# w_in in one load, wo in four, x in five pieces and a mask used as a view, in a single-token attention and gated-MLP kernel

## The chip, the cores and the metric

The kernel runs on one core of a Trainium2 chip. The metric is device microseconds of one execution; lower is better. Three executions of the kernel before gave 126.82 to 126.93 us, median 126.91.

## The reference

One token `x` of 576 features is normalized, and two branches read it; both are added to `x`.

```python
xn = layernorm(x)                                   # [1, 1, 576]
# A: attention over the last W = 4096 positions of a cache
q = (xn @ wq).reshape(1, 1, 32, 128)                # 32 query heads
k, v = k_cache[:, :, -4096:, :], v_cache[:, :, -4096:, :]   # 16 heads, each for two query heads
a = softmax(q @ k.T * 128 ** -0.5) @ v
A = a.reshape(1, 1, 4096) @ wo                      # wo [4096, 576]
# B: gated MLP
z = gelu(xn @ w_in)                                 # w_in [576, 4608]
z1, z2 = z[..., :2304], layernorm(z[..., 2304:])
B = (z1 * (w_sp * z2 + b_sp)) @ w_out               # w_out [2304, 576]
out = x + A + B
```

All inputs are bf16. The window of K and V is 32 MiB, and with the four weight matrices the kernel reads 50.96 MB.

## The kernel before

The order of the instructions on each engine is the order in which the code issues them (`tc.manual_schedule()`); semaphores are put in by the framework.

**Loads.** All big loads are issued by SP, in one order: wq (two row groups, then seven), K0, K1, w_in (seven, then two), K2, V0, K3, V1, V2, V3, w_out, wo in five pieces. K and V are loaded in four groups of four heads, 4 MiB each, 32,768 bytes on each of the 128 partitions. The weights are seen as half rows: `rows(slot, src, name, lo, n, at)` (L74) loads `n` row blocks per partition from block `lo`, either into a new tile of the pool `big` with the tag `slot`, or (with `at`) into part of a tile that is there. Four tags, `a` to `d`, are four buffers, each as large as the largest tile of its tag; a load into a buffer waits until all readers of the tile before it are done:

- `a`: wq's seven rows, w_in's seven rows, V1, then `ends[0]` (w_out and the last wo pieces)
- `b`: K0, K2, V2
- `c`: K1, V0, V3
- `d`: `rest` (wq's first two rows, at 4096 w_in's last two), K3, then `ends[1]` (the first wo pieces)

SP issues in order, so a load that waits holds back the loads behind it. Each load signals one of eight DMA semaphores, which are given out in turn over SP's and ACT's loads; a load waits for the last load that used its semaphore.

**x.** ACT issues the loads of `x` into `xrow` (three pieces of 192 elements, L114) and of the scalars w_sp and b_sp into `spb` (L116, L117).

**Setup.** DVE and POOL build masks from an identity. `cm` (L145) marks, per partition, two by two classes; `dmask` (L147) is the same repeated 128 times along the free dimension, 128x512 fp32, written by POOL.

**The chain from x.** DVE spreads `xrow` into `xtw` (L184) once all pieces are there, PE turns it into a column, DVE and POOL normalize it into `XT` (L209 to L212). PE multiplies wq (L220), waiting before that in its order for `spb` (L213). `qps` goes through `q_rep` (L231, L229) and L237 to `Qb` (L248).

**Groups.** For each of the four groups and each half `c`, `keys` (L264) transposes K on DVE, four instructions of 128x1024 fp32, and `scores` (L271) multiplies on PE. `sm_a` takes the maximum on DVE and the exponentials on ACT (L298), `sm_b` transposes them (L309) and copies them (ACT, L312), `pv` (L335) multiplies by V, `norm` (L345, L349) picks each head's own quarter by `dmask` and adds, `y_mms` and `y_copy` put the result into `Y`. `z_mms` (L371) multiplies w_in, in 162 small matmuls between the scores of groups 1 and 2.

**The end.** PE adds `x`, then w_out's 18 row blocks (`hv`), then wo's 32 row blocks (`Y`) into two accumulators (L471, four matmuls a row block); the group 3 result `Y` comes between w_out's second and third part. Then DVE and ACT copy the accumulators to `res`, and ACT writes it out.

Of the kernel before, what the change touches and what calls it, by code (L numbers as in the profile page):

```python
# [8 lines left out]
FP32 = mybir.dt.float32  # L9
BF16 = mybir.dt.bfloat16  # L10
ALU = mybir.AluOpType
# [3 lines left out]
D = 576  # L15
HQ = 32
HKV = 16
DH = 128
# [8 lines left out]
NR = 98  # L27
NF = FH // 128
QW = D // 4
XP = D // 3  # L30
EPS = 1e-5
SCALE = DH ** -0.5
GELU_C = 0.7978845608028654
NS = 9
# [3 lines left out]
def kernel(  # L38
# [14 lines left out]
    nc = tc.nc  # L53
    P = nc.NUM_PARTITIONS
# [4 lines left out]
    const = ctx.enter_context(tc.tile_pool(name="const", bufs=1))  # L59
# [11 lines left out]
    x_flat = A_x.flatten_outer_dims()  # L71


    def rows(slot, src, name, lo, n, at=None):  # L74

        w = src.shape[1]
        if at is None:
            t = big.tile([P, n * w], BF16, name=f"{name}{lo}", tag=slot)[:]
        else:
            t = slot[:, at:at + n * w]  # L80
        v = t.rearrange("p (s c) -> p s c", c=w)
        nc.sync.dma_start(v, src.rearrange("(p s) c -> p s c", p=P)[:, lo:lo + n, :])  # L82
        return [(lo + s, v[:, s, :]) for s in range(n)]

    def load_kv(slot, src, g, name):

        t = big.tile([P, TP * DH], BF16, name=f"{name}{g}", tag=slot)
        nc.sync.dma_start(t[:], src[0, GK * g:GK * g + GK, SK - W:SK, :].rearrange("h (r t) d -> r h (t d)", t=TP))
        return t[:].rearrange("p (t d) -> p t d", d=DH)

    wq_h = A_wq.rearrange("r (e c) -> (r e) c", e=2)
    win_h = B_w_in.rearrange("r (e c) -> (r e) c", e=2)
    K, V = {}, {}
    rest = big.tile([P, TP * DH], BF16, name="rest", tag="d")
    wq_sb = rows(rest, wq_h, "wq", 0, 2, 0) + rows("a", wq_h, "wq", 2, 7)
    K[0] = load_kv("b", A_k_cache, 0, "k")
    K[1] = load_kv("c", A_k_cache, 1, "k")
    win_sb = rows("a", win_h, "win", 0, 7) + rows(rest, win_h, "win", 7, 2, 4096)
    K[2] = load_kv("b", A_k_cache, 2, "k")
    V[0] = load_kv("c", A_v_cache, 0, "v")  # L100
    K[3] = load_kv("d", A_k_cache, 3, "k")
# [3 lines left out]
    ends = [big.tile([P, TP * DH], BF16, name=f"end{n}", tag="ad"[n]) for n in range(2)]  # L105
    wout_sb = rows(ends[0], B_w_out, "wout", 0, NF, 0)
    wo_sb = []
    for n, t, at in ((14, 1, 0), (9, 1, 14), (6, 0, NF), (2, 0, NF + 6), (1, 0, NF + 8)):
        wo_sb += rows(ends[t], A_wo, "wo", len(wo_sb), n, at * D)


    xrow = const.tile([1, D], BF16, name="xrow")
    for n in range(3):
        nc.scalar.dma_start(xrow[:, XP * n:XP * (n + 1)], x_flat[:, XP * n:XP * (n + 1)])  # L114
    spb = const.tile([1, 2], BF16, name="spb")
    nc.scalar.dma_start(spb[:, 0:1], B_w_sp.flatten_outer_dims()[0:1, 0:1])  # L116
    nc.scalar.dma_start(spb[:, 1:2], B_b_sp.flatten_outer_dims()[0:1, 0:1])  # L117
# [24 lines left out]
    cm = const.tile([P, 2, 2], FP32, name="cm")  # L142
    idc = ident[:].rearrange("p (q u y e) -> p u q y e", q=4, u=2, e=2)
    for e in range(2):
        nc.vector.tensor_reduce(out=cm[:, :, e], in_=idc[:, :, :, :, e], op=ALU.add, axis=mybir.AxisListType.XY)  # L145
    dmask = const.tile([P, 4, DH], FP32, name="dmask")
    nc.gpsimd.tensor_copy(dmask[:], cm[:].rearrange("p u e -> p (u e)").unsqueeze(2).to_broadcast([P, 4, DH]))  # L147
    ohm = const.tile([P, 8], FP32, name="ohm")
    nc.vector.tensor_reduce(out=ohm[:], in_=ident[:].rearrange("p (v y e) -> p y v e", y=8, e=2), op=ALU.add,
                            axis=mybir.AxisListType.XY)  # L150
# [17 lines left out]
    for n in range(2):  # L168
        t = ps_s.tile([P, 2, 512], FP32, name=f"S{n}")
        nc.vector.memset(t[:], 0.0)  # L170
        S.append(t)
    ops = ps_o.tile([P, 512], FP32, name="ops")
# [12 lines left out]
    for j in range(NS):  # L185
# [8 lines left out]
        out=junk[:], in0=x_col[:], in1=x_col[:], scale=1.0, scalar=0.0,  # L194
        op0=ALU.mult, op1=ALU.add, accum_out=stat[:, 1:2],
# [10 lines left out]
                            op0=ALU.subtract, op1=ALU.mult)  # L206
# [135 lines left out]
    def norm(g):  # L342
        d = st[g]
        om = work.tile([P, 4, DH], FP32, name=f"om{g}", tag="om")
        nc.vector.scalar_tensor_tensor(out=om[:].rearrange("p c d -> p (c d)"), in0=ops[:],  # L345
                                       scalar=d["rs"][:, 0:1], in1=dmask[:].rearrange("p c d -> p (c d)"),
                                       op0=ALU.mult, op1=ALU.mult)
        on = work.tile([P, DH], FP32, name=f"on{g}", tag="on")
        nc.vector.reduce_sum(on[:], om[:].rearrange("p c d -> p d c"), axis=AXX)  # L349
        d["on"] = on  # L350
# [67 lines left out]
    def tail(g):  # L418
        recip(g)
        norm(g)  # L420
        y_mms(g)
        y_copy(g)
# [17 lines left out]
    for n, pool in enumerate((ps_a, ps_b)):  # L440
        t = pool.tile([P, 512], FP32, name=f"acc{n}", tag="ab"[n])
# [77 lines left out]
```

## Time and profile before

| | |
|---|---|
| median of three executions | 126.91 us |
| profiled execution | 126.97 us, of which span 125.1 us |
| HBM read | 50.96 MB, 407 GB/s over the span |
| PE, weight loads, DVE, ACT, POOL busy | 70.2, 30.4, 78.6, 43.2, 7.2 us |
| SP's DMA queue, share of 16 DMA engines | 95.3% |
| granted TensorE clock, mean | 0.754 |

A line of the groups or of the timeline gives start and duration in microseconds, the engine, the line of the source, the operation, output and inputs, shape, and how many instructions are merged; in brackets stands the idle time ahead of it and what ended that. PEld are weight loads, which run beside matmuls. `SPq` and `ACTq` are the engines' own DMA instructions. The rows of tenths cut the span into 40 slices of 3.1 us.

### The profile page before, as it was taken

The page shows a single profiled execution, that of the slowest core. Times are in us where ns is not written, and L with a number is a line of the kernel's source. Part 1 is how long each engine was busy: PE and PEld are TensorE (multiplying, and loading weights), DVE is VectorE, ACT ScalarE, POOL GpSimd, SP SyncE. Part 2 cuts the span into 40 slices and gives each one's busy share as a digit, 9 for nine tenths or more (in the row PEclk, how much of TensorE's full clock was granted, in tenths as well). Part 3 has the DMA queues.
Part 4 walks back from the last instruction along what each step waited for, and adds up shares of the span by engine and source line. Part 5 has one row for each costly group of instructions (what it writes and reads, how often), then busy time and mean ns, then how long its engine had stood idle before and what let it go on. Part 6 is the DMA issues. An engine that isn't in the chain of part 4 may idle for free.

```text
span 125.1 us, 1826 instructions
## 1 busy us (share of the span) xinstructions
PE 70.2 (56%) x728; PEld 30.4 (24%) x728; DVE 78.6 (63%) x152; ACT 43.2 (34%) x101; POOL 7.2 (6%) x21
## 2 busy tenths in 40 slices
PE   0012841009886659999580991059892931059972
PEld 0011201001101002999100031002212311026961
DVE  6845135899699976509999367999938359003200
ACT  2100011000000974998079009608701941940000
POOL 2972000000000000000000000000000100000000
PEclk9999997555599958655568599558997555555999
DMA  4999899998999999898999989899998989999960
GB/s 113 507 422 440 363 503 409 430 482 356 498 389 433 385 482 471 377 492 341 492 430 419 471 367 487 359 482 440 409 482 356 492 374 453 414 434 409 413 248 0
DMA packets 2613, 51.06 MB, mean 408 GB/s; under 512 B 300, under 2 KB 430, under 8 KB 686
## 3 DMA queue, kind: packets, MB, share of 16 engines
q1 hardware_dynamic: 2592, 50.96, 95.3%
q8 instruction: 5, 0.08, 0.2%
q14 instruction: 2, 0.02, 0.0%
q10 hardware_dynamic: 14, 0.00, 0.0%
HBM read 50.96 MB, written 0.00 MB: 407 GB/s over the span
## 4 chain that ended last, share of the span: by engine, by line
DMA 62%; DVE 30%; PE 4%; SPq 1%; issue 1%; ACT 0%; DVEq 0%
DMA k<-in_A_k_cache_dram 36%; DMA end<-in_A_wo_dram 25%; DVE kT L264 22%; DVE pt L309 4%; PE S L271 3%; SPq L82 1%; DVE mx L292 1%; DVE on L349 1%; DVE om L345 1%; PE acc L471 0%; PE yps L356 0%; DVE rs L326 0%; ACT res L487 0%; DVE mt L281 0%; DVE mb L287 0%
## 5 line engine op out<-in xcount | busy, mean ns | idle before, releaser
L271 PE MATMUL S<-kT,Qb 128*8 128x512 bf16 x128 | 32.4, 1145 | 23.2 <-DVE kT L264 22.7
L264 DVE STREAM_TRANSPOSE kT<-k 128x1024 f32<-128x1024 f32 x32 | 36.8, 1207 | 6.2 <-DMA k<-in_A_k_cache_dram 6.2
L298 ACT ACTIVATE pz<-S,nm 32x1024 bf16<-32x1024 f32 x16 | 19.2, 1198 | 34.0 <-DVE nm L295 21.1
L312 ACT COPY PT<-pt 32x128 f32<-32x128 f32 x64 | 19.9, 311 | 16.5 <-DVE pt L309 15.8
L335 PE MATMUL ops<-v,PT 128*32 128x512 bf16 x128 | 11.0, 506 | 6.8 <-ACT PT L312 6.8
L271 PEld LDWEIGHTS <-Qb 128*8 128x8 bf16 x128 | 3.6, 96 | 44.9 <-issue 35.4
L309 DVE STREAM_TRANSPOSE pt<-pz 128x1024 f32<-128x1024 f32 x8 | 9.4, 1210 | 0.8 <-ACT pz L298 0.8
L345 DVE SCALAR_TENSOR_TENSOR om<-ops,rs,dmask 128x512 f32<-128x512 f32 x4 | 3.0, 751 | 10.5 <-PE ops L335 10.3
L371 PEld LDWEIGHTS <-win 128*128 128x128 bf16 x126 | 7.9, 166 | 2.0 <-issue 2.0
L371 PE MATMUL zps<-XT,win 128*128 128x2 bf16 x126 | 8.0, 202 | 0.0
L292 DVE TENSOR_REDUCE mx<-S 128x1 f32<-128x1024 f32 x4 | 4.9, 1216 | 4.0 <-PE S L271 3.9
L335 PEld LDWEIGHTS <-PT 128*32 128x32 bf16 x128 | 3.8, 118 | 11.4 <-ACT PT L312 6.9
L229 ACT CAST q_rep<-qps 128x512 bf16<-128x512 f32 x2 | 1.2, 585 | 14.9 <-DVE q_rep L231 14.9
L410 POOL TENSOR_TENSOR mz<-mz,mhalf 128x1 f32<-128x1 f32 x1 | 0.6, 553 | 84.9 <-DVE mz L409 84.9
L186 PE MATMUL ps_x<-ones_b,xtw 1*128 1x1 bf16 x9 | 0.4, 162 | 8.9 <-DVE xtw L184 8.9
L471 PE MATMUL acc<-end,Y 128*2 128x144 bf16 x128 | 4.5, 226 | 0.9 <-DMA end<-in_A_wo_dram 0.8
L231 DVE CAST q_rep<-qps 128x512 bf16<-128x512 f32 x2 | 1.4, 692 | 4.9 <-PE qps L220 4.2
L487 ACT CAST res<-acc 2x144 bf16<-2x144 f32 x1 | 0.3, 270 | 12.0 <-PE acc L471 12.0
L471 PEld LDWEIGHTS <-Y 128*2 128x2 bf16 x128 | 4.1, 84 | 1.2 <-issue 1.2
L356 PE MATMUL yps<-on,sel 128*32 128x32 f32 x32 | 2.0, 210 | 4.1 <-DVE on L349 4.1
L349 DVE TENSOR_REDUCE on<-om 128x128 f32<-128x512 f32 x4 | 4.2, 1043 | 0.1
L486 DVE CAST res<-acc 2x144 bf16<-2x144 f32 x1 | 0.3, 295 | 5.7 <-PE acc L471 5.7
(96 smaller groups left out, 57.6 us busy)
## 6 DMA issues: line engine op xcount, KB each, us to landing
k<-in_A_k_cache_dram SPq DMA_DIRECT2D x4, 4096.0 KB
v<-in_A_v_cache_dram SPq DMA_DIRECT2D x4, 4096.0 KB, 25.4
win<-in_B_w_in_dram SPq DMA_DIRECT2D x1, 4032.0 KB, 26.9
wq<-in_A_wq_dram SPq DMA_DIRECT2D x1, 3584.0 KB, 12.8
end<-in_B_w_out_dram SPq DMA_DIRECT2D x1, 2592.0 KB, 22.3
end<-in_A_wo_dram SPq DMA_DIRECT2D x1, 2016.0 KB
end<-in_A_wo_dram SPq DMA_DIRECT2D x1, 1296.0 KB
rest<-in_B_w_in_dram SPq DMA_DIRECT2D x1, 1152.0 KB
```

What stands on the lines that cost most here:

```text
L264: nc.vector.transpose(dst[:, 1024 * n:1024 * (n + 1)], src[:, 1024 * n:1024 * (n + 1)])
L271: nc.tensor.matmul(S[g % 2][32 * x:32 * x + 8, c, :], lhsT=Qb[:, GK * g + x, be].rearrange("p a h -> p (a h)"), rhs=kv[:, be // 2, be % 2, x],
L292: nc.vector.tensor_reduce(out=mx[:, 0:1], in_=s[:], op=ALU.max, axis=mybir.AxisListType.XY)
L298: nc.scalar.activation(pz[lo:hi, :, :, x, :], s[lo:hi].rearrange("p a (t r e) -> p (a t) r e", r=8, e=2), ACT.Exp, bias=nm[lo:hi, 0:1], sc ...
L309: nc.vector.transpose(dst[:, 1024 * n:1024 * (n + 1)], src[:, 1024 * n:1024 * (n + 1)])
L312: nc.scalar.copy(PT4[32 * a:32 * a + 32, :, x, :], pt[32 * x:32 * x + 32, :, 2 * a:2 * a + 2])
L335: nc.tensor.matmul(ops[32 * q:32 * q + 32, :], lhsT=d["PT"][:, t0 // 2:t0 // 2 + 2].rearrange("p t x h e -> p (t x h e)"), rhs=V[g][:, t0: ...
L345: nc.vector.scalar_tensor_tensor(out=om[:].rearrange("p c d -> p (c d)"), in0=ops[:], scalar=d["rs"][:, 0:1], in1=dmask[:].rearrange("p c ...
L349: nc.vector.reduce_sum(on[:], om[:].rearrange("p c d -> p d c"), axis=AXX)
L356: nc.tensor.matmul(yps[32 * g:32 * g + 32, :], lhsT=sel[:, dq, :], rhs=d["on"][:, 32 * dq:32 * dq + 32], start=(dq == 0), stop=(dq == 3), ...
L371: nc.tensor.matmul(zps[:, :, t], lhsT=wt[:, t, :], rhs=XT[:, s, :], start=(s == 0 and t == 0), stop=(s == NS - 1 and t == NF - 1), skip_gr ...
L471: nc.tensor.matmul(acc[n], lhsT=lhs[:, col, 1 - r:3 - r], rhs=wv[:, QW * (2 * r + n):QW * (2 * r + n + 1)], start=False, stop=(last and r ...
```

## The change

w_in is loaded in one load of nine row blocks into buffer `a`, which grows to 41,472 bytes per partition; `rest` then holds only wq's two rows. wo is loaded in four pieces of 19, 9, 3 and 1 row blocks, the first two into buffer `d` and the others behind w_out in buffer `a`, where five of 14, 9, 6, 2 and 1 were loaded before. `x` is loaded in pieces of 120 elements, four and one of 96. `dmask` is no tile any more but a view of `cm` with a step of zero along the 128 elements, and the product in `norm` reads that view. Nothing is computed otherwise, and the order of the instructions on each engine is unchanged but for these.

```diff
-XP = D // 3
+XP = 120
...
-    win_sb = rows("a", win_h, "win", 0, 7) + rows(rest, win_h, "win", 7, 2, 4096)
+    win_sb = rows("a", win_h, "win", 0, NS)
...
-    for n, t, at in ((14, 1, 0), (9, 1, 14), (6, 0, NF), (2, 0, NF + 6), (1, 0, NF + 8)):
+    for n, t, at in ((19, 1, 0), (9, 1, 19), (3, 0, NF), (1, 0, NF + 3)):
         wo_sb += rows(ends[t], A_wo, "wo", len(wo_sb), n, at * D)
...
-    for n in range(3):
-        nc.scalar.dma_start(xrow[:, XP * n:XP * (n + 1)], x_flat[:, XP * n:XP * (n + 1)])
+    for lo in range(0, D, XP):
+        nc.scalar.dma_start(xrow[:, lo:min(lo + XP, D)], x_flat[:, lo:min(lo + XP, D)])
...
-    dmask = const.tile([P, 4, DH], FP32, name="dmask")
-    nc.gpsimd.tensor_copy(dmask[:], cm[:].rearrange("p u e -> p (u e)").unsqueeze(2).to_broadcast([P, 4, DH]))
+    dmask = cm[:].rearrange("p u e -> p (u e)").unsqueeze(2).to_broadcast([P, 4, DH])
...
-        nc.vector.scalar_tensor_tensor(out=om[:].rearrange("p c d -> p (c d)"), in0=ops[:],
-                                       scalar=d["rs"][:, 0:1], in1=dmask[:].rearrange("p c d -> p (c d)"),
-                                       op0=ALU.mult, op1=ALU.mult)
+        nc.vector.scalar_tensor_tensor(out=om[:], in0=ops[:].rearrange("p (c d) -> p c d", c=4),
+                                       scalar=d["rs"][:, 0:1], in1=dmask, op0=ALU.mult, op1=ALU.mult)
```

## The prediction

> **What bounds the kernel now.** I read the page's slices first, then the chain that ended last, then the end of the timeline, then the trace's record of single DMA packets and semaphore landings.
>
> ```profile
> DMA  4999899998999999898999989899998989999960
> q1 hardware_dynamic: 2592, 50.96, 95.3%
> DMA k<-in_A_k_cache_dram 36%; DMA end<-in_A_wo_dram 25%; DVE kT L264 22%; DVE pt L309 4%; PE S L271 3%; SPq L82 1%; DVE mx L292 1%; DVE on L349 1%; DVE om L345 1%; PE acc L471 0%; PE yps L356 0%; DVE rs L326 0%; ACT res L487 0%; DVE mt L281 0%; DVE mb L287 0%
> ```
>
> The DMA row has no hole between the first and the last two slices, and q1 (SP's queue) fills 95.3% of 16 engines' span. The packet record makes that sharper: summed over 2.0 to 122.0 us only 0.92 us of one 16-engine stretch is idle, nearly all of it after 120 us. The chain names K's load and the transposes only because SP issued loads behind them; each load was queued well before the stream reached it. So the body is bytes over rate, and the change moves no bytes. What can move the time is the overhead per load, a hole in the stream, and what follows the last bytes.
>
> ```profile
> 117.25 2.97 PEld L471 LDWEIGHTS <-Y 128*2 128x2 bf16 x93
> 121.14 1.60 PE L471 MATMUL acc<-end,Y 128*2 128x144 bf16 x36 [0.77 <-DMA end<-in_A_wo_dram]
> 122.17 0.36 PEld L471 LDWEIGHTS <-Y 128*2 128x2 bf16 x11 [0.26 <-issue]
> 122.81 0.27 ACT L487 CAST res<-acc 2x144 bf16<-2x144 f32 x1 [11.98 <-PE acc L471]
> ```
>
> PE does 23 row blocks of wo from 117.25 in 2.97 us (0.129 each), waits for the six-row piece (landed 121.10), waits again for the two-row piece (122.13), and does the last block after 122.41, when the one-row piece lands. The engines finish unevenly: of the 16 landings of the six-row piece ten lie at 119.4 to 119.9 and four at 120.9 to 121.1. Each late engine carried one 16,384-byte packet of q8 (instruction loads, at 37.4, 57.2, 76.6, 100.7 us), which put it back some 1.4 us. The fifth, at 120.1, hits another engine, which lands last.
>
> **Two loads fewer.** w_in's 32,256 + 9,216 bytes per partition become one of 41,472, and five wo loads become four. Median landing to median landing, one load takes 9.70 us for 32,768 bytes per partition, 9.57 for 32,256, 2.73 for 9,216, 2.06 for 6,912, 0.36 for 1,152. A line through 32,768 and 1,152 leaves 0.02 us per load beyond its bytes, so two loads are worth 0.04 us. The other bound is the single packet: 1,213 ns for 32,768 bytes, 58 ns for 1,152, which leaves 16 ns a packet; eight packets per engine and load make 0.13, two loads 0.26. I take 0.04, because the landings include overlap of successive packets. No packet over 32,768 bytes is in the trace; if it were cut in two, the price is that of before, so 0.
>
> **K3 no longer waits for z_mms.** Slot d then holds only two rows of wq. K3 was issued at 59.69 and was needed when V0's bytes ended, near 65. Hidden already: zero. V1 now waits for all z_mms in slot a; it waited behind K3 for the same event.
>
> **x in five pieces.** This is the part with length. All x and spb loads go to one DMA engine, each as one data packet and one semaphore packet, and there they take turns with SP's packets.
>
> ```profile
> 0.73 1.09 ACTq L114 DMA_DIRECT2D xrow<-in_A_x_dram  x3
> 7.55 1.34 DVE L184 COPY xtw<-xrow 1x1152 bf16<-1x1152 bf16 x1 [1.42 <-DMA xrow<-in_A_x_dram]
> 11.81 0.16 PE L213 MATMUL ps_x<-spb,ones_b 1*128 1x2 bf16 x1 [1.34 <-DMA spb<-in_B_b_sp_dram]
> 23.74 9.13 DVE L264 STREAM_TRANSPOSE kT<-k 128x1024 f32<-128x1024 f32 x8 [0.51 <-DMA k<-in_A_k_cache_dram]
> 56.49 4.62 DVE L264 STREAM_TRANSPOSE kT<-k 128x1024 f32<-128x1024 f32 x4 [4.61 <-DMA k<-in_A_k_cache_dram]
> ```
>
> Packets of q10 start at 1.745 (piece 0), 4.94 and 4.96 (piece 1 and its semaphore), then one per turn, 1.065 us apart, behind one 28,672-byte packet of wq each: 6.02, 7.10, 8.17 and on to 11.36. Two more pieces are four more turns, 4 x 1.065 = 4.26 us, so x is complete at 7.42 + 4.26 = 11.68. spb's last lands near 16.2 (the last two turns behind 1.21 us packets of K), still before XT is wanted at 12.80 + 4.26 = 17.06. wq has then landed, so qps loses its 0.2 wait: Qb ends 3.9 later, at 27.1. The first transposes, which sat ready for K0 at 23.74, begin 3.4 late. Of that 1.07 goes in K1's wait (33.94 becomes 36.3), and the other 2.3 in the 4.61 us that DVE waited for K2. What is left comes through ACT: its exponentials of group 1 end at 61.4, where DVE wanted them at 61.04. From there the compute chain runs 0.35 late to the end: Y near 117.45 instead of 117.11. On the queue, K2 is issued at 36.3 (needed 45), V0 at 47.7 (55), V1 at 62 (74), wo at 89.8 (109.7): no hole.
>
> By the Trainium skill's page "DMA: Bandwidth & Descriptors", section "Queues, rings and completion order", an engine drains a whole packet of some 9 to 17 descriptors from one ring before it switches. The trace agrees for the first load alone (eight 8,192-byte packets pass before piece 1); by that rule x would be complete some 26 us late (a rival below).
>
> **Semaphores.** Eight DMA semaphores go round in program order, and a load waits for the last user of its own. With two more ACT loads, wq's seven rows wait for x's piece 0 (landed 2.06; issue to first packet is 1.0 us at the start, so its bytes are ready at 3.1, before the first load runs out at 4.92), K0 for wq's two rows (5.50; needed 13.7), K1 for piece 1 (5.46; needed 23). Nothing on the path, by 1.8 us in the nearest case.
>
> **The view of the mask.** POOL loses a copy of 0.61 us that ended 80 us before its use. The four products on DVE (751 ns for 512 fp32) read the same count with a zero step. No row has such an operand on DVE's product; bounds from 0 to, say, the reduce over a strided view, 1,043 ns: +0.3 us on Y. I take 0, the operation and the PSUM operand being the same.
>
> **The end, summed.** wo's pieces of 19, 9, 3, 1: a block costs 0.341 us of stream (2.73 / 8). The 19-row piece lands on the late engines at 115.93 + 5 x 0.341 = 117.6, about where Y is ready; PE is through it at 120.1. The 9-row piece lands at 119.04 + 1.7 = 120.75, less 0.04. PE: 36 matmuls to 121.9, twelve for the three-row piece (on the late engines at 121.8) to 122.3, the last block then or after its landing, 122.1 to 122.4 as the last q8 packet falls. End of the last matmul at 122.62 to 122.84, against 122.78: from -0.16 to +0.06, mid -0.05. With the stream's saving counted inside, I forecast -0.1: 126.97 of the profiled execution (125.1 of span and 1.87 around it) becomes 126.87, and at the median of 126.91, 0.06 lower, 126.81. A measurement here tells about 0.2%, 0.25 us, from nothing.
>
> **Rivals.**
> Faster: the packet row is right (0.26 instead of 0.04) and the fifth q8 packet, requested 0.4 us later with Y, comes after its engine is done, so the last landing is that of the other four, 122.18 instead of 122.41. Together some -0.45: 126.45. For it: the fit of packet durations is straight. Against: the landings. Chance 0.30, with lesser forms that still pass 0.25.
> Slower, x later still: PE needs 128 x 0.0323 + 0.2 = 4.3 us from Y; Y may come 0.7 us later than I have it before PE ends after the stream. If piece 1's semaphore also takes a turn of its own, x is 1.07 later, the chain is 1.4 late at the end, and the end moves to 123.0: +0.25; two turns more, +1.3. So 127.2 to 128.2. The pair at 4.94 speaks against it. Chance 0.15.
> Slower, the first wait: piece 0 went out 4 ns after the first SP packet (1.745 against 1.741). Were it caught behind the eight packets it would land near 5.3, wq would start at 6.5 instead of 4.92, and a hole of 1.5 us in the stream gives 128.4. Chance 0.06.
> Whole bursts on the ring: x complete at 33 us instead of 7.4, w_in issued near 43 and moving at 44 on a queue dry since 33, and K2, at 58.7, after w_in's end at 56.3: holes of 11 and 3.4 us, 141 us. Piece 2 at 6.02 speaks against it. Chance 0.02.
> The forecast, within 0.25 us: 0.47.
>
> So faster 0.30, same 0.47, slower 0.23. The likeliest case's own range is 126.65 to 127.1. Low end 126.4 by the faster case; the high end takes in the one-turn case and part of the next, 127.5; the first wait and whole bursts are left out.
>
> **What would show it.** Right: q10 packets of x to 10.3 us and xtw at 11.8; first transposes at 27; no slice of DMA under 8 before the end; w_in's landing 0.0 to 0.1 earlier against K1's; PE at wo in three stretches, from 117.6, 120.7 and without a wait after. Wrong: a dip in the DMA row in the second slice (the first wait), PE still on wo more than 0.6 us after the last landing (the compute chain), or a landing of the one-row piece under 122.0.

## The result, and the profile after

The changed kernel takes 127.3 us (median of 17 executions, 126.98 to 128.07) against 126.89 us (126.69 to 127.3) of the kernel before, timed beside it on the same chip. The ratio is 1.0042, with a 95% interval of 1.0025 to 1.0058: slower by 0.3 to 0.7 us. The forecast was 126.81 us, in a range of 126.4 to 127.5, no difference that could be told from nothing. The executions scatter far more than before: nine lie at 126.98 to 127.3 us, eight at 127.42 to 128.07. The profiled one is the fastest of them (126.98 us, span 125.1), so this profile shows the cause in its mildest form; an experiment below (x5_on_before) shows it in full. One execution in all the series below, of x5_on_before, took 129.28 us, over 1.5% above the fastest of its kernel, and is left out of times and ratios.

The page of the changed kernel, the rows that were shown of before:

```profile
DMA  4999998999999988998989999899998989999960
q1 hardware_dynamic: 2304, 50.96, 95.2%
DMA k<-in_A_k_cache_dram 33%; DMA end<-in_A_wo_dram 25%; DVE kT L263 22%; DMA rest<-in_A_wq_dram 4%; DVE pt L308 4%; PE S L270 3%; PE acc L469 1%; DVE mx L291 1%; DVE on L347 1%; DVE om L344 1%; PE yps L354 0%; DVE rs L325 0%; ACT res L485 0%; DVE mt L280 0%; DVE mb L286 0%
```

Between the first and the last two slices none of DMA is under 8, as before, and SP's queue has lost 288 packets (two loads of 128 data and 16 semaphore packets) without a change of its share. What is new is in the chain: `rest`, the first load of wq, with 4%. The timeline of the changed kernel shows why that load now releases something:

```profile
0.74 1.69 ACTq L114 DMA_DIRECT2D xrow<-in_A_x_dram  x5
1.97 0.33 SPq L82 DMA_DIRECT2D wq<-in_A_wq_dram  x1
5.69 1.26 SPq L88 DMA_DIRECT2D k<-in_A_k_cache_dram  x2
7.73 1.34 DVE L183 COPY xtw<-xrow 1x1152 bf16<-1x1152 bf16 x1 [1.59 <-DMA xrow<-in_A_x_dram]
11.99 0.16 PE L212 MATMUL ps_x<-spb,ones_b 1*128 1x2 bf16 x1 [1.33 <-DMA spb<-in_B_b_sp_dram]
14.89 3.15 PE L219 MATMUL qps<-wq,XT 128*2 128x512 bf16 x28 [0.88 <-DMA wq<-in_A_wq_dram]
24.55 9.13 DVE L263 STREAM_TRANSPOSE kT<-k 128x1024 f32<-128x1024 f32 x8 [0.37 <-DMA k<-in_A_k_cache_dram]
56.64 4.62 DVE L263 STREAM_TRANSPOSE kT<-k 128x1024 f32<-128x1024 f32 x4 [4.48 <-DMA k<-in_A_k_cache_dram]
```

The same two SP rows in the timeline of the kernel before, and then the waits of SP's queue in the changed kernel (time in total, how often, the longest):

```profile
1.17 0.42 SPq L82 DMA_DIRECT2D wq<-in_A_wq_dram  x1
1.64 1.30 SPq L88 DMA_DIRECT2D k<-in_A_k_cache_dram  x2
```

```profile
SPq L82 <- DMA xrow<-in_A_x_dram: 0.8, 1, 0.8
SPq L88 <- DMA rest<-in_A_wq_dram: 3.4, 1, 3.4
```

wq's seven rows are queued at 1.97 us instead of 1.17, because their semaphore is now x's piece 0's; K0 and K1 go out at 5.69 instead of 1.64, behind the end of the first load. Both waits were in the prediction, priced at nothing. The first of them is the loss, as the experiments below show.

The record of single packets shows what becomes of it. Before, wq's 128 packets of 28,672 bytes take 1,062 ns each, every one of them: 135.94 us in all. The first load's packets end at 4.84 to 5.23 on the 16 engines, and wq's begin at 4.79 to 5.23. In the changed kernel the first load's packets end at 4.89 to 5.34, but one engine takes up wq only at 5.94, and four packets take longer, up to 1.19 us. That engine stays behind: wq's slowest landing is 14.85 (median 13.88), K0's 24.53 (23.56).

In this execution it costs nothing in the end. A packet's record names no engine, but each packet starts within some nanoseconds of the end of the one before it on its engine, so an engine can be followed. The late one carries no instruction load (q8, the 16,384-byte packets of the prediction) and ends w_out at 110.38; four engines that carried one each end it at 110.76 to 110.90, and those are the last at the end.

### The profile page after: what moved, and what is told of

Same layout as the page of the kernel before. It is cut to its first block, busy times and chain, and to the rows that moved or that the text cites. A ratio compares the mean times of both kernels' runs of the same rounds, so it can differ in the third digit from the quotient of the medians.

```text
span 125.1 us, 1826 instructions
## 1 busy us (share of the span) xinstructions
PE 70.2 (56%) x728; PEld 30.3 (24%) x728; DVE 78.5 (63%) x152; ACT 43.1 (34%) x101; POOL 6.6 (5%) x20
## 4 chain that ended last, share of the span: by engine, by line
DMA 62%; DVE 30%; PE 5%; issue 1%; ACT 0%; SPq 0%; DVEq 0%
DMA k<-in_A_k_cache_dram 33%; DMA end<-in_A_wo_dram 25%; DVE kT L263 22%; DMA rest<-in_A_wq_dram 4%; DVE pt L308 4%; PE S L270 3%; PE acc L469 1%; DVE mx L291 1%; DVE on L347 1%; DVE om L344 1%; PE yps L354 0%; DVE rs L325 0%; ACT res L485 0%; DVE mt L280 0%; DVE mb L286 0%
## 5 line engine op out<-in xcount | busy, mean ns | idle before, releaser
L369 PEld LDWEIGHTS <-win 128*128 128x128 bf16 x162 | 10.1, 169 | 1.9 <-issue 1.9
L369 PE MATMUL zps<-XT,win 128*128 128x2 bf16 x162 | 10.2, 202 | 0.0
L344 DVE SCALAR_TENSOR_TENSOR om<-ops,rs,cm 128x512 f32<-128x512 f32 x4 | 3.0, 751 | 10.5 <-PE ops L334 10.3
```

Of the source, the lines that this page charges most:

```text
L344: nc.vector.scalar_tensor_tensor(out=om[:], in0=ops[:].rearrange("p (c d) -> p c d", c=4), scalar=d["rs"][:, 0:1], in1=dmask, op0=ALU.mult ...
L369: nc.tensor.matmul(zps[:, :, t], lhsT=wt[:, t, :], rhs=XT[:, s, :], start=(s == 0 and t == 0), stop=(s == NS - 1 and t == NF - 1), skip_gr ...
```

## The experiments

Each was timed in five rounds beside the kernel before, whose median lay between 126.83 and 126.94 us. Ratios are to its executions, with 95% intervals; they aren't the quotient of the two medians. "Queued" is the start of SP's DMA instruction.

### Which part of the change

**x3_on_after: three pieces of x again.** Theory: the moved semaphores are the loss; rivals: the five pieces' own packets, the wo pieces, w_in's single load.

```diff
-XP = 120
+XP = D // 3
```

> The changed kernel with x in three pieces again; all else as changed. Theory 1 (first wait): with two ACT loads fewer, wq's seven rows no longer share a semaphore with x's piece 0 and are issued near 1.2 us without a wait; the time goes back to 126.9 (126.6 to 127.1) and its spread back to that of before (some 0.6 us between lowest and highest, against 1.1). Theory 2 (the cost lies in the 41,472-byte packets of w_in or in wo's four pieces): it stays at 127.3.

126.98 us (126.84 to 127.11, 12 executions), 1.001 [1.0002, 1.0019]. Its timeline has wq back at its old place:

```profile
1.16 0.42 SPq L82 DMA_DIRECT2D wq<-in_A_wq_dram  x1
1.63 1.28 SPq L88 DMA_DIRECT2D k<-in_A_k_cache_dram  x2
```

No execution is over 127.11: the pieces of x carry the loss but for 0.1%, and the scatter with it.

**x5_on_before: only the five pieces**, in the kernel before (the diff above, reversed).

> The kernel before with x in five pieces and nothing else. Theory 1: wq waits for piece 0, as in the changed kernel; 127.3 with single executions to 128. Theory 2: no change, 126.9.

128.14 us (127.06 to 128.44, 8 executions), 1.0083 [1.0057, 1.0109]. The profiled execution took 128.19 us, with the loss in full; rows of its timeline:

```profile
1.99 0.33 SPq L82 DMA_DIRECT2D wq<-in_A_wq_dram  x1
5.48 1.25 SPq L88 DMA_DIRECT2D k<-in_A_k_cache_dram  x2
121.87 0.92 PE L471 MATMUL acc<-end,Y 128*2 128x144 bf16 x24 [0.44 <-DMA end<-in_A_wo_dram]
123.24 0.65 PE L471 MATMUL acc<-end,Y 128*2 128x144 bf16 x12 [0.45 <-DMA end<-in_A_wo_dram]
123.95 0.27 ACT L487 CAST res<-acc 2x144 bf16<-2x144 f32 x1 [12.36 <-PE acc L471]
```

PE's last twelve matmuls begin at 123.24, behind a wait for wo, and `res` follows at 123.95 (122.81 before). The loss was there from the start: the median landing of wq is 0.64 us later than before, that of K0 0.66, that of K1 0.71, and the last piece of wo lands at 123.55 instead of 122.41. What the stream loses near 5 us stays lost, because every engine carries an equal part of each later load and the one that is furthest behind ends last.

**after_spb_pool: five pieces, but the two `spb` loads on GpSimd's queue.** Its loads don't take part in the turn of the eight semaphores, so wq and K0 wait for nobody.

```diff
-    nc.scalar.dma_start(spb[:, 0:1], B_w_sp.flatten_outer_dims()[0:1, 0:1])
-    nc.scalar.dma_start(spb[:, 1:2], B_b_sp.flatten_outer_dims()[0:1, 0:1])
+    nc.gpsimd.dma_start(spb[:, 0:1], B_w_sp.flatten_outer_dims()[0:1, 0:1])
+    nc.gpsimd.dma_start(spb[:, 1:2], B_b_sp.flatten_outer_dims()[0:1, 0:1])
```

> The changed kernel, x still in five pieces, but the two scalars of spb are loaded from POOL's queue, so that ACT has five loads and wq shares no semaphore with piece 0. Theory 1: 126.9 or a little less, narrow spread. Theory 3 (five pieces cost by their own turns on the one DMA engine, not by the wait): 127.3 as changed.

127.13 us (126.93 to 127.26, 12 executions), 1.0019 [1.001, 1.0029]; wq queued at 1.17, its packets 135.99 us in all. With five pieces and without the wait the executions over 127.3 are gone. The 0.2% that is left is 0.1% more than with three pieces; here x does take its turns, and the chain from it starts nearly as late as forecast (shown in the part on the prediction). Whether that is the 0.1% isn't shown.

**wo4_on_before and wo4_again: only the four pieces of wo**, the same kernel twice.

```diff
-    for n, t, at in ((14, 1, 0), (9, 1, 14), (6, 0, NF), (2, 0, NF + 6), (1, 0, NF + 8)):
+    for n, t, at in ((19, 1, 0), (9, 1, 19), (3, 0, NF), (1, 0, NF + 3)):
```

> The kernel before with wo in pieces of 19, 9, 3 and 1 and nothing else. Theory 1: within 0.15 us of 126.9. Theory 2: up to 127.3.

126.98 us (126.77 to 128.19, 12 executions), 1.0021 [0.9999, 1.0043]; two executions were at 128.04 and 128.19. The profiled one, at 127.18, has no late load (wq queued at 1.15); the two have no trace.

> wo in 19, 9, 3 and 1 on the kernel before, a second time: two of twelve executions were at 128.0 and 128.2, the others at 126.8 to 127.2. If the pieces of wo bring the loss now and then by themselves, there will be some again; if those two were chance of the chip at large, all will be near 126.9.

127.01 us (126.85 to 127.13, 11 executions), 1.0005 [0.9997, 1.0014], with no such execution. No difference is shown; the two of the first series stay unexplained.

**win9_view: only w_in's single load and the view** (the changed kernel with three pieces of x and five of wo).

> The changed kernel with x in three pieces and wo in five: w_in in one load and the mask as a view alone. If what was left over (126.98 with wo in four, against 126.83) is of wo's pieces: 126.85. If it is of the 41,472-byte rows or the view: 127.0.

126.96 us (126.88 to 127.16, 12 executions), 1.0004 [0.9996, 1.0013]: no difference.

### Which of the two waits

The kernel before, in which a small DVE memset touches a load's buffer, so that the load waits for DVE; x stays in three pieces. The first touches wq's seven rows, the second K0, the third both.

```diff
+    wq_t = big.tile([P, 7 * 2048], BF16, name="wq2", tag="a")
+    nc.vector.memset(wq_t[:, 0:2], 0.0)
+    wq_sb = wq_sb + rows(wq_t, wq_h, "wq", 2, 7, 0)
```

```diff
+    k0_t = big.tile([P, TP * DH], BF16, name="k0", tag="b")
+    nc.vector.memset(k0_t[:, 0:2], 0.0)
+    nc.sync.dma_start(k0_t[:], A_k_cache[0, 0:GK, SK - W:SK, :].rearrange("h (r t) d -> r h (t d)", t=TP))
```

**wq_late.** 

> The kernel before (x in three pieces, nothing waits on a shared semaphore early) with one more small DVE memset on the buffer of wq's seven rows, so that SP issues that load near 2.1 us instead of 1.17; K0 and K1 follow at once. Theory A (wq queued late, after the first load is already running, starts badly on some engines): a spread to 128, packets of wq over 1.06 us. Theory B (K0 and K1 issued at 5.5 us, beside wq's packets, disturb them): 126.9, as before.

127.94 us (127.67 to 129.08, 6 executions), 1.0092 [1.0062, 1.0121]. **k0_late.** 

> The kernel before with a small DVE memset on K0's buffer, so that K0 and K1 are issued near 5.7 us instead of 1.64; wq is issued at 1.17. Theory B: a spread to 128, packets of wq over 1.06 us from 5.5 us on. Theory A: 126.9.

126.79 us (126.68 to 127.07, 11 executions), 0.9992 [0.9982, 1.0001]. **both_late.** 

> Both memsets: wq near 2.1 and K0 and K1 near 5.7 us, the issue times of the five-piece kernels, with x in three pieces and no wait on x. If the issue times alone make the loss: 127.3 to 128.2 with single executions as low as 127. If the turns of x's packets have a part in it: 126.9.

128.03 us (127.41 to 128.33, 6 executions), 1.0073 [1.0054, 1.0092]. The SP rows in the timelines of wq_late and of k0_late (of k0_late without K1's, which follows at 6.34):

```profile
2.08 0.33 SPq L82 DMA_DIRECT2D wq<-in_A_wq_dram  x1
2.46 1.25 SPq L88 DMA_DIRECT2D k<-in_A_k_cache_dram  x2
```

```profile
1.15 0.42 SPq L82 DMA_DIRECT2D wq<-in_A_wq_dram  x1
5.68 0.61 SPq L158 DMA_DIRECT2D k<-in_A_k_cache_dram  x1
```

wq late by itself makes the whole loss, without any change to x; K0 late by itself makes none.

**x4_on_before: x in four pieces** (`XP = D // 4`), which moves each wait by one semaphore less: wq isn't held (queued at 1.15), K0 waits for piece 0 (1.98), K1 for the first load.

> The kernel before with x in four pieces: six ACT loads, so that wq has a free semaphore, K0 waits for piece 0 (near 2.0 us) and K1 for the first load (5.5 us). Theory A: 126.9. Theory B: between, or as with five pieces.

127.03 us (126.88 to 127.34, 12 executions), 1.0011 [1.0002, 1.0021]; wq's packets 135.98 us. One piece more costs at most 0.27 us; the second, by which wq gets the wait, costs the rest.

### What a late wq meets

From the packet records of the profiled executions (us): when wq's seven rows are queued, when the last engine ends the first load, the sum of wq's 128 packets and the longest, the end of wq's last packet, the end of the last data packet, and that execution's time.

| kernel | queued | first load ends | sum | longest | wq ends | data ends | time |
|---|---|---|---|---|---|---|---|
| before | 1.17 | 5.23 | 135.94 | 1.06 | 13.70 | 121.96 | 126.97 |
| k0_late | 1.15 | 5.25 | 135.95 | 1.08 | 13.73 | 122.00 | 126.73 |
| after_spb_pool | 1.17 | 5.12 | 135.99 | 1.11 | 13.62 | 121.84 | 127.26 |
| wq_mid | 1.44 | 5.34 | 135.94 | 1.06 | 13.82 | 121.95 | 126.86 |
| after | 1.97 | 5.34 | 136.26 | 1.19 | 14.55 | 121.91 | 126.98 |
| x5_on_before | 1.99 | 5.12 | 145.99 | 1.97 | 14.87 | 123.07 | 128.19 |
| wq_late | 2.08 | 5.59 | 142.26 | 2.04 | 14.59 | 122.81 | 127.67 |
| both_late | 2.08 | 5.33 | 145.17 | 2.01 | 14.77 | 123.13 | 128.33 |
| wq_late_act1 | 2.08 | 5.36 | 145.28 | 2.04 | 14.73 | 122.78 | 127.89 |
| wq_late_x1 | 2.08 | 5.28 | 141.99 | 1.89 | 14.74 | 123.08 | 128.31 |
| wq_later | 2.60 | 5.25 | 140.22 | 1.45 | 14.79 | 123.14 | 128.2 |

A load queued by 1.44 us is taken up without a gap, packet after packet at 1,062 ns; in all the traces with wq queued so early and this split, the sum is at most 136.05 us and no packet is over 1.17. Queued at 1.97 to 2.60 us, its packets between 5 and 8 us take up to twice that, 4 to 10 us more in all (0.3 to 0.6 per engine) in every profiled execution that was long, and even in the changed kernel's short one, one engine ends wq 0.7 us after the next. How much of that shows in the time depends on what the late engine carries later. In wq_later the engine that ends K0 at 24.47, 0.7 us after the next, is the one that carries the instruction load at 37.7; it ends w_out at 112.08, 0.9 after the next, and is the last of all at 123.14. In the changed kernel's profiled execution the late engine carried none, and nothing was lost. That this makes the scatter between executions is argued from two traces and not shown.

The packets of x show that on their engine SP's ring is then empty: three pieces go through in one burst (5.09 to 5.15 us in the changed kernel, 4.74 to 4.79 in x5_on_before), where before each waited for one packet of SP's. The page "DMA: Bandwidth & Descriptors" of the Trainium skill, section "Queues, rings and completion order", has an engine drain some 9 to 17 descriptors of a ring before it switches; here only the first load's eight packets per engine, which all pass before x's second piece, would fit that. From wq on it takes one packet in turn when both rings are filled and as many as there are when the other is empty.

The first loads of the kernels of the table look alike in one point: the first 16 or so of their 8,192-byte packets take 0.3 to 1.5 us, most later ones 0.31. So packets are stretched in two places where a ring may only just be filling. That this is why, and whether the engine waits there for descriptors, isn't in the traces; it is argued.

**wq_mid: the memset earlier**, so that wq is queued at 1.44.

> The kernel before with a small DVE memset on the buffer of wq's seven rows that ends near 1.5 us, so that this load is issued near 1.6 us, between 1.17 (no loss) and 1.97 (loss). A1: part of the executions lose, or none, at a lead of 3.3 us; A2, where the first packets start at 1.73: no loss.

126.84 us (126.73 to 127.25, 12 executions), 0.9994 [0.9986, 1.0003]: no loss. The border lies between 1.44 and 1.97. This kernel's code is moved about as wq_late's is, memset and all, so that isn't what costs there.

**Is it the lead to the end of the load before?** after_wq3 makes the first load longer in the changed kernel, wq1_on_before makes it shorter in the kernel before (one row and eight). The diff is that of after_wq3.

```diff
-    wq_sb = rows(rest, wq_h, "wq", 0, 2, 0) + rows("a", wq_h, "wq", 2, 7)
+    wq_sb = rows(rest, wq_h, "wq", 0, 3, 0) + rows("a", wq_h, "wq", 3, 6)
```

> The changed kernel with wq split three and six rows instead of two and seven: the wait for x's piece 0 stays (issue near 1.97 us), but the first load lasts 1.6 us longer, to some 6.5 us. Theory A1 (the second load needs a lead of over 3 us before the first runs out): the loss goes, 127.0 with a narrow spread, and wq's packets take their usual time. Theory A2 (a load queued after the first has started to move is always picked up badly): 127.3 or more, as changed.

127.01 us (126.9 to 127.3, 12 executions), 1.001 [1.0001, 1.0018]: wq queued at 1.98, the first load at its end at 6.01 to 6.52, and all 128 packets, now of 24,576 bytes, at 912 ns. With the late load unchanged, a microsecond more of cover takes the loss away, but for the 0.1% that x3_on_after has as well.

> The kernel before with wq split one and eight rows: the second load is still issued near 1.17 us, before the first moves, but the first runs out near 3.3 us, a lead of 2.1. A1: a loss as in the five-piece kernels, 127.3 to 128. A2: 126.9.

126.76 us (126.56 to 127.38, 12 executions), 0.9992 [0.998, 1.0003]. The first load ends at 3.49 to 3.79, 2.3 us after wq is queued at 1.15, less than the 2.9 us that the changed kernel has, and nothing is lost. Some packets are stretched, to 1.56 us at most, 1.3 us in all. So a lead of 3 us is not needed everywhere.

**wq3_late: rows 3 + 6 and x in three pieces in the changed kernel, wq held to 3.35 us by the memset.**

> The changed kernel with x in three pieces, wq split three and six rows, and a small DVE memset on the buffer of the six rows, so that they are issued near 3.4 us; the first load runs out at 6.0 to 6.5 us, a lead of 2.7. A3 (a load that is queued while the engines are already at work needs a lead of about 3 to 4 us, one queued before they start needs about 1): a loss as with wq_late, 127.5 to 128. A4 (only something in the first 5 us of a run is disturbed): 127.0 as the same split issued at 1.98 with a lead of 4.1.

127.06 us (126.96 to 127.4, 11 executions), 1.0013 [1.0004, 1.0022], and in its timeline:

```profile
3.35 0.33 SPq L82 DMA_DIRECT2D wq<-in_A_wq_dram  x1
```

The first load ends at 6.01 to 6.46, 2.65 us later; every packet of wq takes 912 to 915 ns. A load that is queued while the engines work is thus ready within 2.65 us here.

**k0_at_11: K0 held to 11.43 us** in the kernel before, 1.8 to 2.4 us before wq runs out.

> The kernel before with a small DVE memset on K0's buffer that ends near 11.2 us, so that K0 and K1 are issued there, 2.1 us before wq's bytes run out at 13.3. A3: a loss again, here at K0's first packets, 127.4 to 128.5. A4: 126.9.

126.96 us (126.83 to 127.42, 12 executions), 1.0007 [0.9997, 1.0017]. K0's 128 packets take 157.01 us instead of 155.27, the longest 1.66: the same sign, 0.1 us per engine, and no loss that can be told.

**Who disturbs the late load?** Three theories were left: ScalarE's loads, which are queued until 2.7 us, delay it (shared queueing); the lead at this hand-over is too short (lead time); or the burst of x's packets does it. wq_late_act1 is wq_late with only piece 0 on ScalarE's queue, pieces 1 and 2 and `spb` on GpSimd's:

```diff
+        q = nc.scalar if n == 0 else nc.gpsimd
+        q.dma_start(xrow[:, XP * n:XP * (n + 1)], x_flat[:, XP * n:XP * (n + 1)])
```

> Before, with wq's seven rows queued near 2.08 us (a memset on DVE holds them back), and ScalarE queueing only x's piece 0; pieces 1 and 2 and spb go out on GpSimd's queue instead. Shared-queueing theory: the late load is picked up late because ScalarE's loads are still being turned into packets until 2.7 us; with one ScalarE load left it is ready sooner than the 2.65 us that wq3_late needed, before the first load runs out at 4.7 to 5.1: all wq packets at 1,062 ns (sum 136.0 us), 127.0 us. Lead-time theory (this hand-over wants the load queued more than 3 us ahead, whoever else queues): packets stretched as in wq_late (sum 142 to 146 us), 127.9 to 128.1.

128.38 us (127.41 to 128.93, 6 executions), 1.0107 [1.0075, 1.0138]. wq_late_x1 has x in one piece and `spb` on GpSimd's queue:

> As wq_late_act1, but x in one piece on ScalarE's queue and only spb on GpSimd's, so that no packet of x stands between the first load and wq on x's DMA engine. Shared-queueing theory: 127.0. Lead-time theory: 127.9 to 128.1. Burst theory (the packets of x that go through in one burst when SP's ring is empty start the stretched packets): 127.0 here whatever wq_late_act1 shows.

128.16 us (127.79 to 128.58, 6 executions), 1.0092 [1.0075, 1.011]. Neither ScalarE's loads nor the burst is the cause: the loss is there without them. wq_later clears 1,024 columns instead of 2, which queues wq at 2.60:

> As wq_late, with the memset longer, so that wq's seven rows are queued near 2.5 us instead of 2.08; x in three pieces and spb on ScalarE as before, the last of them queued by 2.7 us. Lead-time theory: the lead to the end of the first load is 2.3 instead of 2.8 us: a longer stall than wq_late, 128.1 to 129. Shared-queueing theory: from 2.65 us after its queueing, 5.15 us, it is ready, no later than in wq_late (5.6), so the loss is no larger: 127.2 to 128.0.

127.83 us (127.24 to 128.2, 6 executions), 1.0066 [1.0046, 1.0086]. A lead shorter by 0.5 us costs no more, so the loss doesn't grow with the lead that is missing, as the lead-time theory would have it. None of the three theories holds.

**What stays open:** why a load that is queued at 2.0 to 2.6 us loses 0.3 to 0.6 us of engine time at the hand-over near 5 us, when one queued at 3.35 for a hand-over at 6.0 loses none. The two differ in the size of the packets on both sides (8,192 and 28,672 bytes against 12,288 and 24,576); that wasn't tried by itself.

## Why the prediction was wrong

**The step that failed** is the paragraph on semaphores: wq's seven rows "wait for x's piece 0", "its bytes are ready at 3.1", "nothing on the path, by 1.8 us in the nearest case". The wait and its releaser were right (piece 0 landed at 1.96, forecast 2.06). The price was wrong: the 1.0 us from issue to first packet came from a load that met 16 idle engines. Here x's engine still found nothing of wq at 5.15, 3.2 us after the issue, and the slowest engine took wq up at 5.94, 4.0 us after it and 0.6 or more after the end of its own first load. No row of the profile before showed a load queued behind a working stream with less than wq's 3.7 us to spare (1.17 to 4.92), so the price should have been bounded, and not set to nothing. It measured 0.8 to 1.5 us where it is the only edit (wq_late, 127.94 against 126.88), and 0.3 in the change (127.3, against 126.98 with three pieces of x). Why the load is taken up so late stays open.

**The range** of 126.4 to 127.5 does take in 127.3, but by luck: its high end stood for a chain from x that ends too late, and x came earlier than forecast. The case that came was left out of it.

**The rival "the first wait"** named the place, wq behind piece 0, and the dip in the second slice. But it took a late piece 0 as its condition, and piece 0 landed at 1.96, earlier than before (2.06); with it in time the rival gave no loss. Its price was 1.5 us in every execution; the changed kernel's loss is 0.3 to 0.7 over all executions, 0.1 in some and 1.2 in one. The second slice shows no dip, since stretched packets count as busy.

**K0 and K1 held to 5.69:** nothing, as forecast (k0_late).

**x in five pieces:** forecast complete at 11.68 by one packet per turn, measured 7.61, because SP's ring was empty and three pieces went in a burst. So Qb and the first transposes were not 3.4 us late: the transposes start at 24.55, 0.8 later, which is K0's own lateness on the slowest engine. Y is written until 117.34, before until 117.11, forecast 117.45. Nothing can be read from that: in the kernels with three pieces of x Y is done between 116.61 (x3_on_after) and 117.57 (wo4_again). The rows of before and of the changed kernel:

```profile
116.89 0.22 DVE L363 CAST Y<-yps 32x32 bf16<-32x32 f32 x1 [0.53 <-PE yps L356]
117.12 0.22 DVE L361 CAST Y<-yps 32x32 bf16<-32x32 f32 x1 [0.63 <-PE yps L354]
```

The working itself holds where wq is in time. In x4_on_before x's packets go at 4.79, 5.86, 6.93 and 8.00. In after_spb_pool, with five pieces and wq queued at 1.17, `xtw` starts at 11.55 (forecast 11.8) and the first transposes at 26.53 (27):

```profile
11.55 1.34 DVE L183 COPY xtw<-xrow 1x1152 bf16<-1x1152 bf16 x1 [4.74 <-DMA xrow<-in_A_x_dram]
26.53 13.63 DVE L263 STREAM_TRANSPOSE kT<-k 128x1024 f32<-128x1024 f32 x12
```

So the forecast for x failed by the same step: it took wq's packets to be there to take turns with.

**w_in in one load:** one 41,472-byte packet takes 1,533 ns, the two of before 1,194 and 347, so eight of them save 0.06 us. The forecast had 0.02 a load and the rival "Faster" 0.13. That 0.13 came from 58 ns for a packet of 1,152 bytes, whose median in the trace is 51: with it the same line leaves 9 ns a packet, 0.07 a load. w_in's median landing comes 12.27 us after K1's, 0.03 sooner than before, within the 0.0 to 0.1 forecast.

**The view of the mask:** nothing, as forecast. The group of the product in the changed kernel, 751 ns for one as before:

```profile
L344 DVE SCALAR_TENSOR_TENSOR om<-ops,rs,cm 128x512 f32<-128x512 f32 x4 | 3.0, 751 | 10.5 <-PE ops L334 10.3
```

**The end** came as summed, in the execution that lost little before it; the timeline of the changed kernel:

```profile
117.85 2.54 PE L469 MATMUL acc<-end,Y 128*2 128x144 bf16 x76
120.97 1.79 PE L469 MATMUL acc<-end,Y 128*2 128x144 bf16 x52 [0.58 <-DMA end<-in_A_wo_dram]
120.97 1.59 PEld L469 LDWEIGHTS <-Y 128*2 128x2 bf16 x51 [0.73 <-issue]
122.83 0.27 ACT L485 CAST res<-acc 2x144 bf16<-2x144 f32 x1 [11.87 <-PE acc L469]
```

PE starts on wo at 117.85 (forecast 117.6), on the 9-row piece at 120.97 (120.7), and doesn't wait after that; its last matmul ends at 122.76 (122.62 to 122.84). The last piece lands at 122.34, before at 122.41. Fewer pieces at the end are a wash, as wo4_again also says (1.0005); the first series, wo4_on_before, had 1.0021 with an interval that takes in 1.

**Not accounted for:** a tenth of a per cent in the changed kernel with three pieces of x (1.001 [1.0002, 1.0019]), which no part shows by itself (win9_view 1.0004 and wo4_again 1.0005, each within the noise, would add up to it); and why the changed kernel scatters less badly than x5_on_before, with wq queued at the same moment.

## What to carry to other kernels

A small load more on any queue that shares the DMA semaphores moves every later load's wait: go through the turn, and see which large load gets which small one's semaphore. Keep the second load of a stream queued right behind the first, since 0.8 us more cost this one up to 1.2 us, and an engine that falls behind there stays behind, as every engine carries an equal part of each later load. And take the time from issue to first packet from a load that met the same conditions; where there is none, bound it.

## What the runs showed of the hardware

- Packets are not of fixed duration: 28,672 bytes took 1,062 ns in a stream that was queued early (single ones up to 1,174) and up to 2,038 ns when the load was queued at 2.08 us, for some three microseconds after the hand-over at 5 us.
- Such a loss is random: the changed kernel's executions lie 0.1 to 1.2 us above the median of before, wq_late's 0.8 to 2.2.
- An instruction load of 16,384 bytes puts its DMA engine behind, some 1.4 us (before: four such engines land wo's six-row piece at 120.9 to 121.1, ten others at 119.4 to 119.9), and adds to what that engine has lost before (wq_later: 0.7 us behind at K0, last of all at 123.14).
- When one ring of a DMA engine is empty, the other's packets go in a burst: six packets of x in 0.06 us, against 1.07 us each in turn.
- A load queued late in mid-stream can cost nothing: K0 queued 1.8 to 2.4 us ahead, 0.1 us per engine and no measurable time.
